# Another order of steps in the later stages of a fused Linformer attention and two-layer kernel on one Trainium2 core

## The chip, the cores and the metric

The kernel runs on one core of one Trainium2 chip. The metric is the device time of one execution in microseconds (us). Engines are called as in the profile: PE (TensorE, matmuls; PEld is its weight loads), DVE (VectorE), ACT (ScalarE), POOL (GpSimd) and SP (SyncE, which here only issues DMAs).

## The reference

Eight batches of an attention with projected keys and values, then two matrix products with a gated activation between them:

```python
k_proj = np.einsum('ks,bhsd->bhkd', E, k)          # b=8, h=8, s=1024, d=64, k=64
v_proj = np.einsum('ks,bhsd->bhkd', F, v)
scores = scale * np.matmul(q, k_proj.transpose(0, 1, 3, 2))
attn = softmax(scores)                              # over the 64 projected keys
x = np.matmul(attn, v_proj)                         # -> (8192 tokens, 512)
h = x @ w_in                                        # 512 -> 2048
g = h * np.clip(h + 3.0, 0.0, 6.0) / 6.0
out = g @ w_out                                     # 2048 -> 512
```

## The kernel before, in words

**Stages.** A batch has 1024 tokens; a stage is 512 of them (t = 0 or 1), so there are 16 stages, named here by batch and t ("5/1" is batch 5, t = 1). Each stage makes the first layer of its own tokens (`g`, 16 blocks of 128 rows) and the second layer of the tokens of the stage ahead of it. The attention of the next batch lies between the matmuls: scores, exponentials and row sums in t = 0, the products with the values in t = 1, and the projection of the batch after that in t = 0.

**Second layer: pairs A and B.** Output rows are made in two pairs, each with seven products of half-size blocks instead of eight (`Pair.step`). A7 is product 7 of pair A, and so on; each is 16 matmuls of 256 columns. Products 7, 2 and 5 go to PSUM tiles `at` and are copied by ACT. Products 6, 1, 3 and 4 add up in this order in one PSUM tile `mm`, and between two of them DVE (ACT after the last) reads the tile into `o_sb`. So the next product of that pair waits for that reading. Product 1 needs the block difference `sb` (DVE), product 3 `sd` (POOL), product 5 `sc` (POOL). N2 and N5 are products 2 and 5 of the next stage's pair A, made a stage early. `o_sb` has three buffers, freed by the store to DRAM.

**First layer from batch 3 on: L0 to L7 and the quarters Q and R.** Half of the blocks of `g` are plain groups (`L` steps, 8 matmuls of 512 columns; ACT makes `r`, DVE makes `g` from `r` and the PSUM tile, line 571). The other half are two quarters made in seven products each (`Quad.step`, 8 matmuls of 256 columns), from sums of `x` blocks that POOL makes (`xc`, `xa`, `xb`, `xd`). Again 6, 1, 3 and 4 add up in one `mm` tile with a DVE subtraction into `qm` (line 136) between them; 7, 2 and 5 go to `at` and are copied by ACT (line 774). Each output goes `qm` -> `r` (ACT, line 783) -> `g` (DVE line 789, or POOL line 787 for products 6 and 1 of R). These parts are put into the queues two steps after the product (`behind_steps(2)`), and the `g` of DVE two more. q3 and q4 are products 3 and 4 of Q, made in the next stage. "gR3" below is the `g` of R3; "gQ1", "gL0" likewise.

**Order.** `QUADS` is the written order of a stage's steps; an engine's work stands in its queue in the order in which the steps issue it. `MADE` says after which step the sums are issued (x: the four sums of x; a: in place in `g`, DVE; b: `sb`; c: `sc`; d: `sd`), `LAST` and `TAIL` are the same for the end, where only the second layer of the last stage is left. The calls of `at(...)` hang the attention onto steps: `scores`, `add_up` (row sums, DVE line 315), `spread` (`sums_turned`, small DVE transposes and adds; `spread_sums`, a DVE reciprocal at line 334 and ten DMAs on SP), `projected` (16 matmuls, then two ACT copies `kp` and, one at each of the next poppable steps, the transposing DMAs on SP and two ACT copies `vp`), and `load_next` (a mark and three DMA issues on POOL).

**PSUM.** There are four `mm` and four `at` tiles; a new tile takes the one that was released longest ago in program order.

The step of a quarter, which the prediction follows most closely (`Quad.step`, without the allocation of its tiles; line 796; `Quad.out` is at line 777, `Pair.step` at line 706, the plan and the loop over the steps from line 856 on):

```python
            self.product(n, self.y if n in (2, 5) else self.x, n in (2, 6))
            if n == 2:
                self.m2 = self.copied("m2", self.y)
            elif n == 5:
                self.m5 = self.copied("m5", self.y)
            elif n == 6:
                sub(self.m7, self.m7, self.x)
                self.out(self.m7, 1, 0, self.engines[0])
            elif n == 1:
                sub(self.m5, self.m5, self.x)
                self.out(self.m5, 1, 1, self.engines[1])
            elif n == 3:
                sub(self.m2, self.x, self.m2)
                self.out(self.m2, 0, 1, self.engines[2])
            else:
                self.out(self.x, 0, 0, nc.vector)
```

Of the kernel before, what the change touches and what calls it, by code (L numbers as in the profile page):

```python
# [15 lines left out]
def kernel(  # L16
# [111 lines left out]
    KH, MH = FO // 2, d_model // 2  # L128
# [100 lines left out]
    class Attention:  # L229
# [38 lines left out]
        def scores(self, j, *allocs):  # L268
            qT = qT_dma[self.b]
            tiles = [alloc() for alloc in allocs]  # L270
            for a in range(2):
                for t in range(NB):
                    for r in range(2):
                        nc.tensor.matmul(tiles[r][t * KP:(t + 1) * KP, a * HT:(a + 1) * HT],  # L274
                                         self.kT[r * D:(r + 1) * D, 2 * j + a, :],
                                         qT[r * D:(r + 1) * D, j, a, t * HT:(t + 1) * HT],
                                         start=True, stop=True)
            return tiles
# [32 lines left out]
        def add_up(self, *js):  # L311
            if self.parts is None:
                self.parts = att.tile([P, KO, 32], f32, tag="parts", name="parts", bufs=1)
            for j in js:
                nc.vector.tensor_reduce(out=self.parts[:, j], op=ALU.add, axis=mybir.AxisListType.X, apply_transpose=True,  # L315
                                        in_=self.aT[j].rearrange("p a r n -> p (a r n)").rearrange(
                                            "p (c i) -> p c i", i=32))
# [283 lines left out]
    xT = x_tile()  # L601
# [235 lines left out]
    for what in "A2 A7 V0 B7 A5 V1 A6 R B2 A1 V2 B5 R A3 B6 V3 A4 B1 R".split():  # L837
# [11 lines left out]
        if what in added:  # L849
            added[what]()  # L850
    xT = x_next
# [3 lines left out]

    ORDER = ("L0 A7 L1 A6 L2 B7 L3 A1 L4 B2 L5 A3 L6 B5 L7 A4 "
             "L8 L9 B6 L10 N2 L11 B1 L12 N5 L13 B3 L14 L15 B4").split()
    QUADS = ("L0 q3 L7 A7 L5 q4 L1 B7 A6 L3 L2 L6 A1 B2 R7 L4 B6 B5 "
             "A3 R2 R6 B1 R5 N2 A4 Q2 R1 Q7 Q6 B3 Q5 R3 Q1 N5 R4 B4").split()
    MADE = {'L1': 'x', 'R2': 'c', 'q3': 'a', 'B2': 'd', 'A6': 'b'}  # L860
    LAST = {'q3': 'ab', 'A6': 'd'}
    ENGINES = ((nc.vector, nc.vector, nc.vector), (nc.scalar, nc.scalar, nc.vector),)
    START = "L0 B3 L1 L2 B4 L3 L4 L5 L6 L7 L8 L9 L10 N2 L11 L12 L13 N5 L14 L15".split()
    TAIL = ("q3 B2 q4 A7 B7 A6 B6 "
             "A1 B5 B1 A3 B3 A4 B4").split()

    second = Attention(2)
# [2 lines left out]
    for b in range(1, B):  # L870
        if b + 1 < B and b < 4:
            x_next = second.xT = x_tile()
        third = Attention(b + 2) if b + 2 < B else None

        plan = {}

        def at(place, *what):
            plan.setdefault(place, []).extend(what)

        def scores(*js):  # L880
            return lambda: second.some_scores(js)

        def values(*js):
            return lambda: second.some_values(*js)

        def add_up(*js):
            return lambda: second.add_up(*js)

        def spread(turned, inverted):
            at(turned, lambda: second.sums_turned())  # L890
            at(inverted, lambda: second.spread_sums())

        if b == 1:
            at((0, "L2"), sums_of_w_in)
            at((0, "L0"), second.projected)
            at((0, "L8"), second.load_next)
            at((0, "N5"), scores(0, 1))
            at((0, "L15"), add_up(0))
            at((1, "L0"), add_up(1))
            at((1, "L1"), scores(2, 3))  # L900
            at((1, "L2"), add_up(2))
            at((1, "L3"), add_up(3))
            spread((1, "B2"), (1, "L5"))
        elif b == 2:
            at((0, "L2"), second.projected)
            at((0, "A4"), second.load_next)
            at((0, "A4"), scores(0, 1))
            at((0, "B6"), scores(2))
            at((0, "L10"), add_up(0))
            at((0, "B1"), scores(3), add_up(1))  # L910
            at((0, "B3"), add_up(2))
            at((1, "A6"), add_up(3))
            spread((1, "A1"), (1, "L4"))
            at((1, "L12"), lambda: sums_in_place(1))
            at((1, "L4"), third.projected)
        elif b + 1 < B:
            if b == 3:
                at((0, "L0"), lambda: sums_in_place(0))
                at((0, "start"), second.load_next)
            at((0, "q3"), scores(0, 1))  # L920
            at((0, "L6"), add_up(0))
            at((0, "L3"), scores(2, 3))
            at((0, "B5"), add_up(1))
            at((0, "R7"), add_up(2))
            at((0, "A4"), add_up(3))
            spread((0, "Q2"), (0, "Q6"))
            if third:
                at((0, "Q2"), lambda: third.projected(pause=False))
                if third.b + 1 < B:
                    at((1, "B1"), third.load_next)  # L930
        if b < 3:
            at((1, "N2"), values(0))
            at((1, "L12"), values(1))
            at((1, "B3"), values(2))
            at((1, "L14"), values(3))
            if b == 1:
                at((1, "B3"), lambda: behind_that(second.recs[1][:1, 0, :1], 3, "q"))
        elif b + 1 < B:
            at((1, "L3"), values(0, 1))
            at((1, "B5"), values(2, 3))  # L940

        def done(place):
            for f in plan.pop((t, place), ()):
                f()

        for t in range(NB):
            if t and 3 < b < B - 1:
                x_next = second.xT = x_tile()
            g = g_tile()
            sums = Sums(g)  # L950
            start = (b, t) == (1, 0)
            pairs = {"A": behind[0], "B": behind[1], "N": Pair(b, t, sums, 0, (b, t) == (B - 1, NB - 1))}
            quads = b > 2
            if quads:
                for i, engines in enumerate(ENGINES):
                    pairs["QR"[i]] = Quad(i, xT, t, g, (b, t) == (B - 1, NB - 1), engines)
            if not start and not quads:
                behind[0].sums.a(KH - left, KH)
            pairs.update({n.lower(): quad for n, quad in before.items()})
            before = {n: pairs[n] for n in "QR" if n in pairs}  # L960
            made = {"a": lambda before=behind[0].sums, lo=KH - left: before.a(lo, KH), "b": behind[0].sums.b,
                    "d": behind[0].sums.d, "c": sums.c, "x": lambda: pairs["Q"].sums(*[pairs[n] for n in "R" if n in pairs])}
            left = 8 if quads else 2
            done("start")
            for what in START if start else QUADS if quads else ORDER:
                n = int(what[1:])

                def sums_made():
                    for op in MADE.get(what, "") if quads else "":
                        made[op]()  # L970

                if what[0] != "L":
                    if what[0] in pairs:
                        pairs[what[0]].step(n)
                    step_done()
                    if quads and what[0] in "LQRB":
                        pop()
                    done(what)
                    sums_made()
                    if what == ("B5" if quads else "N5" if start else "B3") and left < KH:  # L980
                        sums.a(0, KH - left)
                    continue
                if b < 4 and t == 0 and n < 2:
                    if n == 0:
                        first_two = TwoGroups(xT, t, g)
                    for fo in range(2):
                        first_two.part(fo, range(n * (KO - 1), KO - 1 + n))
                    if n == 1:
                        first_two.out()
                else:  # L990
                    first_group(xT, t, g, n, behind_steps(1) if quads and n >= KH else now)
                step_done()
                pop()
                if not quads and n == KH - 1:
                    sums.c()
                if not quads and not start and n == 0:
                    behind[0].sums.b()
                    behind[0].sums.d()
                done(what)
                sums_made()  # L1000
            while soon and not quads:
                step_done()
            behind = [pairs["N"], Pair(b, t, sums, 1, (b, t) == (B - 1, NB - 1))]
        assert not plan, plan
        second, xT = third, x_next
# [40 lines left out]
```

## Time and profile before

| what | us |
|---|---|
| median of 3 runs (lowest to highest) | 485.64 (485.25 to 485.98) |
| the profiled execution | 486.51 |
| its span, first to last instruction | 484.7 |
| PE busy in the span | 472.8 (98%) |
| DVE busy | 368.6 (76%) |
| ACT busy | 299.1 (62%) |
| POOL busy | 266.6 (55%) |

The granted TensorE clock is 1.00 in every stretch. The first `L0` of batch 3 starts at 191.14, that of 3/1 at 220.95, of 4/0 at 249.18, 4/1 at 277.51, 5/0 at 305.73, 5/1 at 334.07, 6/0 at 362.29, 6/1 at 388.90, 7/0 at 416.78 and 7/1 at 442.64; the tail starts at 468.50, and the last matmul at 480.52 ends it.

A row of the timeline gives the start, the time taken, the engine, the line, the operation, what it writes and reads, and how many instructions the row merges; in brackets stands the idle time ahead of it and who ended it. A matmul row's end is modelled, and the next row may start before it; the distance between the starts of two steps is what a step costs.

### The profile page before, as it was taken

How to read it: one execution, taken by the hardware profiler on the slowest of the kernel's cores; microseconds unless marked ns; L12 is line 12 of the kernel's file. 1: busy time of each engine (PE TensorE's matmuls, PEld its weight loads, DVE VectorE, ACT ScalarE, POOL GpSimd, SP SyncE). 2: the span in 40 equal slices, each digit the busy share in tenths (PEclk: the TensorE clock that was granted, in tenths of full speed). 3: DMA queues.
4: the chain of work that ended last, by engine and by line, in shares of the span. 5: the costliest groups of instructions: out<-in, count | busy, mean ns of one | idle time of the engine just before them, and what ended most of it. 6: DMA issues, size and time to landing. Idle time of an engine off the chain costs nothing.

```text
span 484.7 us, 15486 instructions
## 1 busy us (share of the span) xinstructions
PE 472.8 (98%) x6690; PEld 357.1 (74%) x6690; DVE 368.6 (76%) x578; ACT 299.1 (62%) x580; POOL 266.6 (55%) x175
## 2 busy tenths in 40 slices
PE   8999999999999999999999999999999999999996
PEld 3554567667676786687788868787697968888896
DVE  3582386678856858879879797998979997968784
ACT  2666587774357454757486755867468665757471
POOL 8624948244135333865694648575475657576510
PEclk9999999999999999999999999999999999999999
DMA  9999999984986969988699495966810171101012
GB/s 164 198 201 207 230 157 210 182 127 92 245 130 119 212 155 217 193 184 152 165 167 184 107 167 137 201 128 124 200 65 23 69 197 47 46 34 57 23 69 88
DMA packets 84597, 68.70 MB, mean 142 GB/s; under 512 B 38320, under 2 KB 70576, under 8 KB 84528
## 3 DMA queue, kind: packets, MB, share of 16 engines
q0 software_dynamic: 33008, 29.36, 39.2%
q1 hardware_dynamic: 51152, 37.83, 32.0%
q8 instruction: 52, 0.85, 0.8%
q10 hardware_dynamic: 368, 0.52, 0.4%
q14 instruction: 17, 0.14, 0.1%
HBM read 71.83 MB, written 16.97 MB: 183 GB/s over the span
## 4 chain that ended last, share of the span: by engine, by line
PE 66%; DVE 18%; DMA 5%; POOL 4%; ACT 3%; issue 2%; SPq 1%; DVEq 0%; ACTq 0%; POOLq 0%
PE mm L206 44%; PE at L206 17%; DVE g L789 5%; DVE g L571 4%; DVE qm L136 2%; DVE g L136 1%; DVE sb L136 1%; PE at L295 1%; DMA qT<-q 1%; DMA g<-in_F_dram 1%; DVE parts L315 1%; DVE o_sb L136 1%; PE at L274 1%; DMA rec<-turned_rows 1%; DVE xT L307 1%
## 5 line engine op out<-in xcount | busy, mean ns | idle before, releaser
L206 PE MATMUL mm<-xT,w_in_sb 128*64 128x512 bf16 (+1 forms) x1568 | 183.5, 369 | 1.6 <-ACT o_sb L738 0.9
L206 PEld LDWEIGHTS <-w_in_sb 128*64 128x64 bf16 x2048 | 116.4, 110 | 58.7 <-issue 9.9
L571 DVE SCALAR_TENSOR_TENSOR g<-r,mm 128x512 bf16<-128x512 f32 x176 | 117.6, 680 | 46.8 <-ACT r L570 46.0
L570 ACT ACTIVATE r<-mm 128x512 f32<-128x512 f32 x176 | 104.4, 598 | 70.6 <-PE mm L206 55.4
L206 PEld LDWEIGHTS <-g 128*64 128x64 bf16 x2048 | 113.4, 110 | 20.8 <-issue 3.6
L136 POOL TENSOR_TENSOR sd<-g,sb 128x1024 bf16<-128x1024 bf16 x28 | 59.0, 2127 | 80.6 <-DVE sb L136 80.6
L133 POOL TENSOR_TENSOR sc<-g 128x2048 bf16<-128x2048 bf16 x14 | 57.0, 4072 | 46.5 <-DVE g L571 34.1
L206 PE MATMUL mm<-w_out_sb,g 128*64 128x256 bf16 (+1 forms) x1088 | 77.7, 285 | 1.0 <-DVE o_sb L136 0.7
L206 PE MATMUL at<-w_sums,g 128*64 128x256 bf16 x896 | 59.2, 273 | 0.0
L700 ACT COPY m<-at 128x256 f32<-128x256 f32 x84 | 31.1, 370 | 33.7 <-PE at L206 29.1
L774 ACT COPY qm<-at 128x512 f32<-128x512 f32 x60 | 34.9, 582 | 25.0 <-PE at L206 18.2
L783 ACT ACTIVATE r<-qm 128x512 f32<-128x512 f32 x60 | 37.8, 630 | 12.3 <-DVE qm L136 12.2
L789 DVE SCALAR_TENSOR_TENSOR g<-r,qm 128x512 bf16<-128x512 f32 x42 | 42.5, 1027 | 2.1 <-ACT r L783 1.9
L136 DVE TENSOR_TENSOR qm<-qm,mm 128x512 f32<-128x512 f32 x40 | 27.3, 686 | 19.6 <-PE mm L206 15.4
L307 DVE TENSOR_TENSOR xT<-at,rec 128x512 bf16<-128x512 f32 x54 | 35.9, 682 | 3.7 <-PE at L295 1.7
L787 POOL TENSOR_TENSOR g<-r,qm 128x512 bf16<-128x512 f32 x18 | 22.9, 1274 | 28.0 <-ACT r L786 27.9
L206 PE MATMUL mm<-w_sums,sb 128*64 128x256 bf16 x480 | 31.4, 273 | 1.3 <-DVE sb L136 1.0
L206 PE MATMUL mm<-w_out_sb,sd 128*64 128x256 bf16 x480 | 31.6, 273 | 1.1 <-POOL sd L136 1.0
L283 ACT ACTIVATE aT<-at 128x512 bf16<-128x512 f32 x52 | 29.3, 598 | 1.9 <-PE at L274 1.9
L206 PEld LDWEIGHTS <-sb 128*64 128x64 bf16 x480 | 26.2, 110 | 5.7 <-DVE sb L136 2.6
L315 DVE TRANSPOSE_TENSOR_REDUCE parts<-aT 128x32 f32<-128x1024 bf16 x24 | 29.6, 1232 | 0.0
L206 PE MATMUL at<-w_out_sb,sc 128*64 128x256 bf16 x448 | 29.4, 273 | 0.0
(115 smaller groups left out, 613.2 us busy)
## 6 DMA issues: line engine op xcount, KB each, us to landing
out_dram<-o_sb SPq DMA_DIRECT2D x60, 256.0 KB, 3.8
rec<-turned_rows SPq DMA_DIRECT2D x48, 256.0 KB, 6.2
k<-in_k_dram POOLq DMA_DIRECT2D x7, 1024.0 KB, 9.7
v<-in_v_dram POOLq DMA_DIRECT2D x7, 1024.0 KB, 15.3
q<-in_q_dram POOLq DMA_DIRECT2D x7, 1024.0 KB, 19.4
w_out_sb<-in_moe_w_out_dram POOLq DMA_DIRECT2D x4, 512.0 KB, 14.8
w_in_sb<-in_moe_w_in_dram POOLq DMA_DIRECT2D x7, 256.0 KB, 9.4
k<-in_k_dram POOLq DMA_DIRECT2D x4, 256.0 KB, 5.8
```

The costliest lines, as they stand in the source:

```text
L133: engine.tensor_tensor(out=out, in0=x, in1=y, op=ALU.add)
L136: engine.tensor_tensor(out=out, in0=x, in1=y, op=ALU.subtract)
L206: nc.tensor.matmul(ps[lo:lo + width], stationary[:, lo:lo + width], moving, **flags)
L283: when(lambda r=r: nc.scalar.activation(aT[:, :, r, :], tiles[r].rearrange("p (a n) -> p a n", a=2), AF.Exp, scale=scale))
L307: when(lambda t=t: nc.vector.tensor_mul(self.xT[:, j, t, :], av[t], rec[:, t]))
L315: nc.vector.tensor_reduce(out=self.parts[:, j], op=ALU.add, axis=mybir.AxisListType.X, apply_transpose=True, in_=self.aT[j].rearrange("p a ...
L570: nc.scalar.activation(r, h_ps, AF.Relu, bias=0.5, scale=1.0 / 6.0)
L571: when(lambda: nc.vector.scalar_tensor_tensor(g[:, fo, :], r, 1.0, h_ps, op0=ALU.min, op1=ALU.mult))
L700: self.copy(m, ps)
L774: nc.scalar.copy(m, y)
L783: nc.scalar.activation(r, h, AF.Relu, bias=0.5, scale=(-1.0 if engine is nc.scalar and not self.last else 1.0) / 6.0)
L789: behind_steps(2)(lambda: nc.vector.scalar_tensor_tensor(g, r3, 1.0, h3, op0=ALU.min, op1=ALU.mult))
```

## The change

It gives another written order to the stages of batches 3 to 7 and to the tail, and hangs sums and attention onto other steps:

```diff
-    QUADS = ("L0 q3 L7 A7 L5 q4 L1 B7 A6 L3 L2 L6 A1 B2 R7 L4 B6 B5 "
-             "A3 R2 R6 B1 R5 N2 A4 Q2 R1 Q7 Q6 B3 Q5 R3 Q1 N5 R4 B4").split()
-    MADE = {'L1': 'x', 'R2': 'c', 'q3': 'a', 'B2': 'd', 'A6': 'b'}
-    LAST = {'q3': 'ab', 'A6': 'd'}
+    QUADS = ("L0 q3 L7 A7 L5 q4 L1 B7 A6 L3 L2 L6 A1 B6 B2 L4 R7 B5 "
+             "R6 R2 B1 A3 R5 Q2 R1 Q7 N2 Q6 A4 R3 B3 Q5 Q1 N5 R4 B4").split()
+    MADE = {'L6': 'x', 'R6': 'c', 'A6': 'b', 'q3': 'a', 'R7': 'd'}
+    LAST = {'q3': 'ab', 'B5': 'd'}
...
-    TAIL = ("q3 B2 q4 A7 B7 A6 B6 "
+    TAIL = ("q3 A7 B2 B7 B6 q4 A6 "
              "A1 B5 B1 A3 B3 A4 B4").split()
...
-            at((0, "q3"), scores(0, 1))
-            at((0, "L6"), add_up(0))
-            at((0, "L3"), scores(2, 3))
-            at((0, "B5"), add_up(1))
-            at((0, "R7"), add_up(2))
-            at((0, "A4"), add_up(3))
-            spread((0, "Q2"), (0, "Q6"))
+            at((0, "L0"), scores(0, 1))
+            at((0, "B6"), add_up(0))
+            at((0, "L6"), scores(2, 3))
+            at((0, "R6"), add_up(1))
+            at((0, "L6"), add_up(2))
+            at((0, "A3"), add_up(3))
+            spread((0, "Q7"), (0, "Q7"))
             if third:
-                at((0, "Q2"), lambda: third.projected(pause=False))
+                at((0, "R5"), lambda: third.projected(pause=False))
                 if third.b + 1 < B:
-                    at((1, "B1"), third.load_next)
+                    at((1, "A3"), third.load_next)
...
-                    if what == ("B5" if quads else "N5" if start else "B3") and left < KH:
+                    if what == ("R2" if quads else "N5" if start else "B3") and left < KH:
...
-                    first_group(xT, t, g, n, behind_steps(1) if quads and n >= KH else now)
+                    first_group(xT, t, g, n, behind_steps(2) if quads and n >= KH else now)
```

The first line of the last two edits is in force only where `left < KH`; with the quarters `left` is 8 and `KH` is 8. The second is in force only for `n >= 8`, and `QUADS` holds L0 to L7 alone. Neither alters an instruction. The number and the shapes of the matmuls stay as they are.

## The prediction

> **What bounds the kernel now.** First the page: PE is busy nearly all the time. (Measured against the runs shown, 0.2%, about 1.0 us, is what can be told from no change.)
>
> ```profile
> span 484.7 us, 15486 instructions
> PE 472.8 (98%) x6690; PEld 357.1 (74%) x6690; DVE 368.6 (76%) x578; ACT 299.1 (62%) x580; POOL 266.6 (55%) x175
> ```
>
> So the order can win only what PE waits. Then I walked PE's timeline from batch 3 on and took the distance between the starts of successive steps. Undisturbed, a pair product or an L group takes 0.87 and a quarter product 0.44 (5/0: starts at 321.42, 322.30, 322.73). What is over is lost:
>
> - 5/1: L0 0.06, q3 (L7 comes late) 0.49, A7 (L5 late) 0.48, B2 (R7 late) 0.24, together 1.27; 3/1 and 4/1 the same.
> - 3/0: 1.13 ahead of A1 and 1.19 within A3. 6/1: 0.28 (L5), 0.30 (A6), 0.33 (R7). 7/0 and 7/1: 0.58 each (half ahead of A1). Tail: 0.27, 0.38 (B1) and 0.89 (B4).
>
> Some 9.8 us in all; switches to attention matmuls (0.1 each) and 0.31 in each `values(2, 3)` stay. The Trainium skill (Trainium Kernel Development and Optimization, Performance Expectations) calls matmul busy time a bad metric, because matmuls are pipelined. The trace agrees: from 200 us on the busy time leaves only 5.2 us idle ahead of the last matmul, less than the sum over starts.
>
> Now who holds PE up at the start of a t = 1 stage; PE, then DVE, then ACT in the same stretch:
>
> ```profile
> 334.07 1.03 PE L206 MATMUL mm<-xT,w_in_sb 128*64 128x512 bf16 x8
> 335.00 0.63 PE L206 MATMUL mm<-xd,w_in_sb 128*64 128x256 bf16 x8
> 335.92 1.05 PE L206 MATMUL mm<-xT,w_in_sb 128*64 128x512 bf16 x8 [0.29 <-ACT o_sb L738]
> ```
> ```profile
> 329.11 0.69 DVE L136 TENSOR_TENSOR qm<-qm,mm 128x512 f32<-128x512 f32 x1 [1.19 <-PE mm L206]
> 330.17 0.69 DVE L136 TENSOR_TENSOR qm<-qm,mm 128x512 f32<-128x512 f32 x1 [0.38 <-ACT qm L774]
> 330.78 0.94 DVE L334 RECIPROCAL inv<-inv 64x128 f32<-64x128 f32 x1
> ...
> 334.87 2.61 DVE L789 SCALAR_TENSOR_TENSOR g<-r,qm 128x512 bf16<-128x512 f32 x2
> ```
> ```profile
> 334.98 0.63 ACT L783 ACTIVATE r<-qm 128x512 f32<-128x512 f32 x1 [0.39 <-DVE qm L136]
> 335.51 0.35 ACT L738 COPY o_sb<-mm 128x256 f32<-128x256 f32 x1
> ```
>
> L7 needs the tile that B4 leaves; B4's copy on ACT (335.51) stands behind the `r` of Q1, which waits for the subtraction after Q1 on DVE. DVE then has gR3 and gQ1 (334.87 to 337.48) ahead of gL0, whose tile L5 needs. DVE is late there because R3, Q5 and Q1 come close together, and in 4/1 ACT's copy after Q5 waits 0.87 for POOL's gR1, which holds the one `qm` buffer of product 5. Two more waits:
>
> ```profile
> 204.45 4.21 POOL L136 TENSOR_TENSOR sd<-g,sb 128x1024 bf16<-128x1024 bf16 x2
> ...
> 208.72 0.63 PE L206 MATMUL mm<-w_out_sb,sd 128*64 128x256 bf16 x8 [0.99 <-POOL sd L136]
> ```
> ```profile
> 480.04 0.42 DVE L136 TENSOR_TENSOR o_sb<-mm,m 128x256 f32<-128x256 f32 x1 [1.50 <-DMA out_dram<-o_sb]
> 480.52 1.06 PE L206 MATMUL mm<-w_out_sb,g 128*64 128x256 bf16 x16 [0.69 <-DVE o_sb L136]
> ```
>
> **Part by part.** Matmuls are the same, so each part is worth the wait that it adds or ends.
>
> *Sums (x, d, c) at other steps: nothing.* On POOL the order stays x, sd, sc, gR6, gR1; x still runs as soon as gR1 and Q5 are done, sd when `sb` is.
>
> *A3 three steps later (behind R6, R2, B1).* In 3/0 POOL reaches sd late (it ends at 208.6). A3 would start at 202.30 + 4x0.87 (A1, B6, B2, L4) + 0.44 (R7) + 0.87 (B5) + 2x0.44 + 0.87 = 208.8: the 1.19 go. The 1.13 ahead of A1 stay: `sb` (3.18 us beside x on POOL) does not move.
>
> *B6 and B2 ahead of L4 and R7.* R7 comes 1.7 us later against the `at` tile that it waits for, and B2 0.9: 0.24 gone in 3/1 to 5/1, 0.33 in 6/1. B6 now needs the `mm` tile of L3 0.9 to 1.7 us earlier; in 4/1 gL3 ends at 288.9 and B6 would start at 289.6: hidden.
>
> *Two-step distances.* Between two products on one tile PE in the stages now has at least 2.2 us of other steps (B3 to B4), where R3 to R4 had 1.3; a DVE reading is 0.33 to 0.68. R1 to Q5 grows from 2.2 to 4.4 us, so ACT's wait for gR1 goes. R6 to Q7 shrinks from 4.4 to 3.9 (more with the projection between): gR6 stands behind sc (4.07) on POOL, and in 7/0 ACT's copy after Q7 waits 1.1 us, with r of R1 and m of N2 behind it; Q6's subtraction is then ready 0.4 later, and Q1 three steps after: nothing for PE.
>
> *Scores, row sums, projection.* scores(0, 1) ahead of q3 instead of behind it cost PE the same 0.56. add_up(2) now stands on DVE right behind scores(2, 3) and waits for two exponentials (0.35 us), with the readings of A1 and B6 behind it, whose next products are 9 and 7 steps off: hidden. The projection at R5 puts its transposes (SP) ahead of A4's store, which now also stands behind the row sums' ten DMAs: the transposes would run from 327.4 to 333.1 and the ten DMAs 7.6 us more (280.30 to 287.91 in 4/1), so it leaves near 341 and lands near 345; its buffer is next written after B6 of the next stage, near 347. load_next after A3 is 0.9 later on POOL, still ahead of gR1, for data used a stage later.
>
> *End of a t = 0 stage (5/0, with PE's times as they would be: R1 ends at 327.0, Q6 at 328.8, Q1 starts at 331.35, the next L0 at 334.0).* Now sums_turned and the reciprocal stand together ahead of Q6's subtraction. DVE from 327.15 without a pause: subtraction after R1 0.60, sums_turned 2.0, reciprocal 0.86, after Q6 0.60 (ends 331.2), after R3 0.60, B3's reading 0.33, gQ6 1.1, after Q1 0.60 (ends 333.8), gR3 1.2, gQ1 1.25: 336.3, where before it was 337.5. ACT's r of Q1 can then run at 333.9, B4's copy ends at 334.8, and L7 wants it at 335.3: 0.49 and L0's 0.06 gone. gL0 ends at 336.9, L5 wants its tile at 337.05. That has no room, so I take half of 0.48. With R7's 0.24 each of 3/1, 4/1 and 5/1 gains 1.03. In 6/0 there is no projection, so PE is there 1.7 us sooner while DVE is not: gQ1 ends 2.55 after the next L0 (2.6 before), so 6/1 keeps all but R7's 0.33; and Q6's subtraction ends 0.1 after Q1 wants to start, 0.2 lost.
>
> *7/0 and 7/1.* At the end of 6/1 nothing of the row sums is in the way: gQ1 ends 1.2 after L0 instead of 2.3, at the end of 7/0 1.8 instead of 2.3; `sb` follows on a DVE without a pause, so A1's wait (0.27) and the ones ahead go: 0.48 and 0.38 of 0.58.
>
> *Tail.* A1 now follows A6 at once and must wait for A6's reading: 0.6 lost. q4 later puts its `g`, and so sd on DVE, behind A1's reading: A3 waits 0.35. But A1's reading no longer stands behind sd (476.04 to 476.41 before), and its store, on whose buffer B3's reading waits, leaves 0.7 sooner; such a store took 3.6 (to 480.04). B4 would end 12.3 after the start of the tail, not 12.9: 0.55 gained.
>
> Sum: 1.19 + 3x1.03 + (0.33 - 0.2) + 0.86 + 0.55 = 5.8 us. The profiled execution (486.51; span 484.7 and 1.8 around it) is 0.87 over the median; the gains are taken from the median: 485.64 - 5.8 = 479.8. Everything that could go gone, 7.9 us, gives 477.7.
>
> **Rivals.**
>
> *DVE stays late (25%).* x starts on POOL 1.1 us sooner against the stage's end, so three DVE operations meet it. Rows: gR3 and gQ1 take 2.42 to 2.61 beside POOL's x, 1.47 at 467.96 with POOL idle. If each is held to the end of a whole POOL operation (1.60) and then takes its own 0.60, DVE's chain ends some 2.8 us later and the stage starts keep their stalls: 1.19 + 3x0.24 + 0.33 + 0.55 = 2.8 gained, 482.9. The Trainium skill (SBUF — State Buffer, Who interferes with whom) gives this rule: a DVE instruction with two SBUF inputs and a GpSimd one that reads SBUF exclude each other for the whole instruction. The rows above show 1.2 each, so less than the worst case.
>
> *Slower: the block of row sums (15%).* 2.86 us of DVE work stand ahead of Q6's subtraction, and Q1 cannot start before that. In 3/0 to 5/0 DVE has 1.3 us to spare ahead of R1, in 6/0 none. From there every us by which DVE falls behind (four add_ups of 1.15 now between L6 and R5, the first behind the exponentials) is a us of PE in each of four stages, and the stage starts stay late. With 1.2 us: 485.64 - 2.8 + 4x1.2 = 487.6; it decides from 0.7 us on. Against it: the chain above, worked out from 5/0's own rows.
>
> *No difference (5%).* The waits only move to the next tile: 485.6.
>
> **Numbers.** The main case has 55%; 479.8 is its time, 477.7 to 482 its own range. Faster by over 0.2% is it and the first rival: 0.80; same 0.05, slower 0.15. The range from 477.9 to 485.0 takes in both, and leaves out the slower rival and a few per cent below.
>
> **What would show it.** In the changed profile: A3 of the first quarter stage without a wait for sd; L7 and L5 of t = 1 stages 0.87 apart from their neighbours; no ACT wait for POOL's gR1; a wait of about 0.6 between A6 and A1 in the tail. Wrong: waits of Q1 for DVE's `qm` in t = 0, or L7 and L5 waiting as now.

## The result and the profile after

The changed kernel takes 491.97 us (median of six runs, 489.43 to 494.18), the kernel before 486.15 in the runs beside it (485.25 to 488.11): the ratio is 1.0117, with a 95% interval of 1.0077 to 1.0158. It is slower by some 5.7 us, where a gain of 5.8 was forecast. The profiled execution took 490.93.

Page of the changed kernel (span, the busy times, the granted clock in 40 slices, then one of the costliest groups and one of the DMA issues):

```profile
span 489.1 us, 15494 instructions
PE 472.5 (97%) x6690; PEld 360.7 (74%) x6690; DVE 367.1 (75%) x578; ACT 298.4 (61%) x580; POOL 265.7 (54%) x175
...
PEclk9999999999999999999899999999989999999999
...
L136 DVE TENSOR_TENSOR o_sb<-m,mm 128x256 f32<-128x256 f32 x60 | 24.1, 408 | 15.6 <-DMA out_dram<-o_sb 9.5
...
out_dram<-o_sb SPq DMA_DIRECT2D x60, 256.0 KB, 4.7
```

PE's busy time is what it was (472.5 against 472.8), so by this page the difference is idle time. A matmul at half clock counts as busy all the same (from 356.63 to 360.04 PE is busy for all of the 3.41 us, at a granted clock of 0.50), so part of it can be slow clock. The group on `o_sb` names a wait of 9.5 us for a DMA (1.5 before, all of it in the tail), the stores' median from issue to landing is 4.7 us (3.8 before), and the clock has two dents. The waits of DVE say how often (total, times, longest):

```profile
DVE o_sb L136 <- DMA out_dram<-o_sb: 9.5, 3, 3.7
```

Three times, one in each of 3/1, 4/1 and 5/1. Counted from the start of one step to the start of the next, as the prediction does, PE loses 5.32 us in 3/1 (2.12 before), 2.84 in 4/1 (2.10) and 5.60 in 5/1 (2.11), and from 191 us to the end 19.8 (15.3). The difference of 4.5 is that of the spans (4.4). Here is 3/1, first DVE's timeline, then PE's:

```profile
231.70 0.69 DVE L307 TENSOR_TENSOR xT<-at,rec 128x512 bf16<-128x512 f32 x1
232.31 0.41 DVE L136 TENSOR_TENSOR o_sb<-m,mm 128x256 f32<-128x256 f32 x1
236.13 0.42 DVE L136 TENSOR_TENSOR o_sb<-m,mm 128x256 f32<-128x256 f32 x1 [3.41 <-DMA out_dram<-o_sb]
236.47 0.68 DVE L307 TENSOR_TENSOR xT<-at,rec 128x512 bf16<-128x512 f32 x1
```
```profile
234.06 0.40 PE L295 MATMUL at<-aT,vp 64*64 64x512 bf16 x2
237.20 1.06 PE L295 MATMUL at<-aT,vp 64*64 64x512 bf16 x6 [2.74 <-DVE xT L307]
238.20 1.06 PE L206 MATMUL mm<-xa,w_in_sb 128*64 128x256 bf16 x8
239.05 1.06 PE L206 MATMUL at<-xT,v_sums 128*64 128x256 bf16 x8
239.90 1.37 PE L206 MATMUL mm<-w_sums,sb 128*64 128x256 bf16 x16
...
241.98 0.60 PE L206 MATMUL at<-xc,w_in_sb 128*64 128x256 bf16 x8
242.42 0.60 PE L206 MATMUL at<-xT,v_sums 128*64 128x256 bf16 x8
```

The reading after B6 wants to write an `o_sb` buffer that a store has not yet emptied. It stands at the head of DVE, so the `xT` of `values(2, 3)` stands behind it, and PE's attention matmuls wait for the `at` tile which that `xT` reads. PE names `xT`, DVE names the store. (Behind the wait R6 and R2, the rows at 238.20 and 239.05, cost 0.85 each, and R5 at 241.98 again the usual 0.44: that is the clock, of which more below.) The cause is one row deeper, in the SP queue. First SP of the changed kernel from the end of 3/0 into 3/1, then of the kernel before (start, time on the queue, DMAs):

```profile
212.28 1.21 SPq L257 DMA_TRANSPOSE kT<-kp  x1
215.36 5.73 SPq L194 DMA_TRANSPOSE qT<-q  x2
221.19 1.00 SPq L337 DMA_DIRECT2D turned_rows<-inv  x2
223.34 5.16 SPq L343 DMA_DIRECT2D rec<-turned_rows  x8
228.59 4.49 SPq L704 DMA_DIRECT2D out_dram<-o_sb  x3
```
```profile
213.71 0.33 SPq L704 DMA_DIRECT2D out_dram<-o_sb  x1
216.57 1.22 SPq L257 DMA_TRANSPOSE kT<-kp  x1
```

Before, A4's store leaves at 213.71, ahead of everything. Now it is the first of the three that leave from 228.59 on, behind three transposes, the two DMAs that write the turned rows and the eight that read them back to all partitions. And it lands late, at 236.0. The DMA view of the changed kernel from 226 to 242 (busy share in 40 slices of 0.4 us) shows why:

```profile
DMA  8999995889999999999999986310000100000000
```

The eight transfers of 256 KB fill the DMA engines until 235.6; the store issued behind them lands 0.4 us later.

### The profile page after: what moved, and what is told of

It is laid out like the page before. It is cut to its first block, busy times and chain, and to the rows that moved or that the text cites. A ratio compares the mean times of both kernels' runs of the same rounds, so it can differ in the third digit from the quotient of the medians.

```text
span 489.1 us, 15494 instructions
## 1 busy us (share of the span) xinstructions
PE 472.5 (97%) x6690; PEld 360.7 (74%) x6690; DVE 367.1 (75%) x578; ACT 298.4 (61%) x580; POOL 265.7 (54%) x175
## 4 chain that ended last, share of the span: by engine, by line
PE 78%; DVE 7%; DMA 7%; ACT 4%; POOL 2%; issue 2%; ACTq 0%; DVEq 0%; POOLq 0%
PE mm L206 55%; PE at L206 19%; DMA out_dram<-o_sb 5%; DMA v<-in_v_dram 2%; PE at L295 2%; DVE g L571 2%; DVE g L789 2%; PE at L274 1%; ACT aT L283 1%; DVE parts L315 1%; DVE qm L136 1%; DVE sb L136 1%; POOL q L103 1%; DVE o_sb L136 1%; ACT r L570 1%
## 5 line engine op out<-in xcount | busy, mean ns | idle before, releaser
L789 DVE SCALAR_TENSOR_TENSOR g<-r,qm 128x512 bf16<-128x512 f32 x42 | 45.3, 1089 | 1.8 <-ACT r L783 1.4
L136 DVE TENSOR_TENSOR o_sb<-m,mm 128x256 f32<-128x256 f32 x60 | 24.1, 408 | 15.6 <-DMA out_dram<-o_sb 9.5
L206 PE MATMUL mm<-w_sums,sb 128*64 128x256 bf16 x480 | 32.6, 280 | 0.9 <-DVE o_sb L136 0.5
```

Of the source, the lines that this page charges most:

```text
L136: engine.tensor_tensor(out=out, in0=x, in1=y, op=ALU.subtract)
L206: nc.tensor.matmul(ps[lo:lo + width], stationary[:, lo:lo + width], moving, **flags)
L789: behind_steps(2)(lambda: nc.vector.scalar_tensor_tensor(g, r3, 1.0, h3, op0=ALU.min, op1=ALU.mult))
```

## The experiments

Theory S is this one: the new place of A4 and of the projection on SP delays A4's store, and the wait for its buffer is the whole loss. Theory K adds that the longest of these waits cost more than their length, since PE's clock falls after them. The rivals, which go by further letters where an expectation names them, are the other new waits that the change could have made: row sums that reach `values(2, 3)` too late, the transposes or the new plan of attention as such, the new order of the products. All ratios are to the kernel before, run on the same chip.

**1. A4's store past SP's queue.** In the changed kernel the store of A4 in t = 0 is issued from ACT.

```diff
+            self.queue = nc.sync
...
-                self.store(0, left if self.final else slice(0, d_model), nc.scalar if self.final else nc.sync)
+                self.store(0, left if self.final else slice(0, d_model), nc.scalar if self.final else self.queue)
...
+                        if quads and t == 0 and what == "A4":
+                            pairs["A"].queue = nc.scalar
                         pairs[what[0]].step(n)
```

> The changed kernel, but in the t = 0 stages the store of A4's rows is issued from ACT's queue instead of SP's. Theory S (the store stands on SP behind the projection's three transposes and the row sums' ten DMAs, so its o_sb buffer comes free late, DVE's reading after B6 of the next stage waits 2.4 to 3.6 us, and PE runs dry at values(2, 3) and then at half clock): those waits and the half clock go, about 12 us of the changed kernel's 491 to 492; about 480, ratio to before 0.985 to 0.992. Rival V (the products with the values wait for their own reciprocals, which the moved row sums bring late): within 1 us of the changed kernel, 491. Rival O (B6 ahead of L4 as such, not the buffer): 490 to 492.

Measured: 481.84 us (480.41 to 482.38), ratio 0.9909 (0.9884 to 0.9934). The wait for `o_sb` is gone, and the clock is 0.999 for the whole span of 480.6. One queue for one store turns the loss into a gain: S holds, and the rivals have nothing left of the loss to explain. What remains of them in the stretch of the loss is 1.02 us on DVE in 3/1, where `xT` waits for `rec`, and 0.64 of it reaches PE.

**2. The late store alone, in the kernel before.** Only the store of A4 moves there, to behind Q6.

```diff
+                send = lambda: self.store(...)
+                send() if self.kept is None else self.kept.append(send)
...
+                        if quads and t == 0 and b < B - 1 and what == "A4":
+                            pairs["A"].kept = []
...
+                    if quads and t == 0 and b < B - 1 and what == "Q6":
+                        for send in pairs["A"].kept:
+                            send()
```

> The kernel before, with one edit: in the t = 0 stages of batches 3 to 6 the store of A4's rows is issued after Q6, behind the row sums' DMAs, and not at A4. Theory S: it leaves SP as late as in the changed kernel (some 9 us after the next L0 and 7 to 8 us to landing), but B6 is 1.7 us later in this order, so DVE's reading waits 0.7 to 1.9 us and part of it reaches PE: 487 to 490, ratio 1.003 to 1.010, the wait of o_sb for the DMA seen in 3/1, 4/1 and 5/1. Rivals V and O: no change, 485.6 to 486.2, ratio 0.998 to 1.002.

Measured: 488.86 (486.79 to 490.05), ratio 1.0051 (1.0032 to 1.0071). The waits of DVE:

```profile
DVE o_sb L136 <- DMA out_dram<-o_sb: 7.1, 4, 2.9
```

One of the four is the tail's old one. At the step behind A3, which needs the tile that the `xT` behind the wait reads, PE loses 0.42, 1.93 and 0.86 in 3/1, 4/1 and 5/1, 3.2 in all, which is near what the ratio gives (2.5 us). The late store is enough to make the kernel before slower, with no other part of the change.

**3. The projection behind A4.** In the changed kernel its transposes are issued at A4, so that the store goes ahead of them.

```diff
-                at((0, "R5"), lambda: third.projected(pause=False))
+                at((0, "A4"), lambda: third.projected(pause=False))
```

> The changed kernel with the projection hung onto A4 instead of R5, so that its three transposes stand on SP behind A4's store; the row sums' ten DMAs stay ahead of it. Theory S: the store leaves 6 to 8 us sooner, the wait goes in all three stages: 480 to 482, ratio 0.986 to 0.993. Rival D (not the queue, but the row sums' broadcasts in flight make the store land in 7.5 us instead of 3.8): a wait of 1 us or more stays in 3/1 to 5/1, 484 to 489. Rival V: 491.

Measured: 480.82 (480.27 to 481.51), ratio 0.9893 (0.9871 to 0.9916), span 478.6. SP, in the place shown above:

```profile
222.26 0.54 SPq L704 DMA_DIRECT2D out_dram<-o_sb  x1
```

The store leaves 6.3 us sooner and no reading waits for it, though it still takes 6.7 us to land, behind the same eight transfers. The transposes are as many as before and run later still (the `qT` ones from 224.30 to 232.33), so they do no harm by themselves.

**4. The row sums behind A4.** The other half of the queue: the reciprocal and the ten DMAs of the row sums move from Q7 to R3, behind A4, while the projection stays at R5.

```diff
-            spread((0, "Q7"), (0, "Q7"))
+            spread((0, "Q7"), (0, "R3"))
```

> The changed kernel with the reciprocal and the row sums' ten DMAs hung onto R3 instead of Q7, so that they stand behind A4's store (and DVE reads Q6 ahead of the reciprocal); the transposes stay ahead. Theory S: the store leaves at the end of the transposes, about 7 us sooner, the wait goes: 480 to 481, ratio 0.986 to 0.992. Rival D: the same. Rival V (reciprocals late): the row sums come later still, so 491 or more.

Measured: 481.18 (480.30 to 481.92), ratio 0.9896 (0.9868 to 0.9924). The store leaves at 221.38, now ahead of the eight transfers, and lands in 2.8 us. To clear either half out of its way is enough. The row sums are read back later here than in the changed kernel (from 224.65 instead of 223.34), and the loss is gone all the same: late row sums are not its cause. They are not free either: DVE's `xT` waits for `rec` three times, 3.1 us in all, and 3/1 takes 28.05 us from L0 to L0, where experiment 3 has 27.23.

**5. The order without the plan.** The changed orders and sums with the hooks of the kernel before, except for `add_up(3)`, which stays at A3.

```diff
-            at((0, "L0"), scores(0, 1))
+            at((0, "q3"), scores(0, 1))
...
-                at((0, "R5"), lambda: third.projected(pause=False))
+                at((0, "Q2"), lambda: third.projected(pause=False))
```

> The changed order of steps, sums and tail with the attention of the kernel before on its old steps (projection and sums_turned at Q2, reciprocal and row DMAs at Q6, scores at q3 and L3; add_up(3) at A3, since A4 now comes after Q2). Theory S: A4 still comes after both, so its store still stands behind transposes and row DMAs: the wait of o_sb for the DMA stays in 3/1, 4/1 and 5/1, 487 to 492, ratio 1.003 to 1.013. Rival P (the new places of the projection and the row sums cause the loss): as fast as with the store freed, 480 to 482.

Measured: 489.88, 491.05 and 493.80, ratio 1.0105 (1.0067 to 1.0143). The fourth execution, the profiled one, took 1236 us and is left out, so there is no trace to read. The new orders and sums are enough for a loss of that size. Theory S has the reason: in the new order A4 stands behind Q2 and Q6, at which that plan puts the projection and the row sums on SP, where in the kernel before it stood ahead of both. That it is the store which costs the time in this run is not shown.

**6. The plan without the order.** The kernel before with the changed hooks.

```diff
-            spread((0, "Q2"), (0, "Q6"))
+            spread((0, "Q7"), (0, "Q7"))
...
-                at((0, "Q2"), lambda: third.projected(pause=False))
+                at((0, "R5"), lambda: third.projected(pause=False))
```

> The kernel before with the new places of the attention alone (scores, add_up, projection at R5, row sums at Q7, load_next at A3), order, sums and tail as before. Theory S: A4 still comes ahead of Q2, where the transposes are issued, and of Q7, so its store leaves in time: no wait of o_sb for a DMA in t = 1; the stage starts wait as before: 485 to 487, ratio 0.998 to 1.003. Rival P (the new places as such cause the loss): 489 to 492, ratio 1.007 to 1.013.

Measured: 487.54 (486.68 to 488.65), ratio 1.0026 (1.0009 to 1.0043). There is no wait for a store in t = 1, but another one appears in each of 3/0 to 6/0, 4.4 us in all. PE and then DVE in 4/0:

```profile
275.81 0.63 PE L206 MATMUL mm<-xb,v_sums 128*64 128x256 bf16 x8 [1.09 <-DVE qm L136]
```
```profile
274.27 0.94 DVE L334 RECIPROCAL inv<-inv 64x128 f32<-64x128 f32 x1
275.14 0.62 DVE L136 TENSOR_TENSOR qm<-qm,mm 128x512 f32<-128x512 f32 x1
```

This is the prediction's slower rival, the block of row sums ahead of Q6's subtraction: 4/0, 5/0 and 6/0 take 1.25 us longer from L0 to L0 than in the kernel before. It exists in the old order, where 1.75 us of other steps lie between Q6 and Q1; in the new one there are 2.6, and no Q1 waits. The ratio lies in the range of theory S (the time, 487.54, is 0.5 above it), but the stage starts do not wait as before, as S had said: 3/1, 4/1 and 5/1 are 1.0 us shorter each and 6/1 0.8, which takes most of the new waits back.

**7. B6 later.** In the changed kernel B6 goes behind B2, L4 and R7, some 2.2 us later, where the buffer is asked for later.

```diff
-    QUADS = ("... A1 B6 B2 L4 R7 B5 "
+    QUADS = ("... A1 B2 L4 R7 B6 B5 "
```

> The changed kernel with B6 moved behind R7 (A1 B2 L4 R7 B6 B5), nothing else: DVE's reading after B6, which waits for the buffer, is asked for 2.2 us later, and the store is as late as in the changed kernel. Theory S: the waits of 2.4 to 3.6 us shrink by 2.2 each, PE waits at most 1.5 us in a stage and keeps its full clock: 482 to 485, ratio 0.992 to 0.998. If the loss came from the store's lateness through another reader than B6's: 490 to 492.

Measured: 483.73 (481.65 to 486.60), ratio 0.9949 (0.9921 to 0.9977). The waits of DVE keep 3.6 us for the store in two places, where 9.5 in three were:

```profile
DVE o_sb L136 <- DMA out_dram<-o_sb: 3.6, 2, 2.0
```

Two of the three waits are left, and shorter: it is a race between landing and asking, and either end moves it. The runs whose mean clock is 0.999 or 1.000 take 481.65 to 483.73, those at 0.996 take 484.8 to 486.6.

**8. The wait kept, the clock kept up.** Fourteen matmuls of no use ahead of `values(2, 3)` in 3/1 and 5/1, so that PE is not idle while it waits for the store.

```diff
+            if b in (3, 5):
+                at((1, "B5"), lambda: busy(14))
             at((1, "B5"), values(2, 3))
```

> The changed kernel with 14 idle matmuls of 128x512 (about 3.0 us, results unused) put ahead of values(2, 3) in 3/1 and 5/1, where PE waits about 2.9 us. Theory K (a wait of 2.7 us and more halves PE's clock for 3.41 us, 1.7 us each, on top of the wait): the matmuls fill the wait, the clock stays at 1.00 there and 3 to 4 us are gained on the changed kernel: 487 to 489, and the runs lie closer together. Without K: no gain or a loss of up to 1 us, 491 to 493.

Measured: 489.21 (488.85 to 490.41), ratio 1.0061 (1.0046 to 1.0076). The windows view from 229 to 245 us (length, busy time of PE, PEld, DVE, ACT and POOL, then the granted clock, the DMA share and GB/s), of the changed kernel and then of this one:

```profile
229.00:245.00 16.00, 13.26 (x196) 11.05 (x194) 9.85 (x18) 6.35 (x13) 11.07 (x7) 0.89 0.50 141
```
```profile
229.00:245.00 16.00, 15.94 (x231) 12.66 (x230) 10.85 (x20) 7.56 (x15) 11.38 (x7) 1.00 0.50 135
```

With the idle time filled (PE's busy time here holds the matmuls of no use) the clock stays at 1.00, and about half of the slowdown is gone though the store is as late (DVE still waits for it three times, 9.0 us in all): K holds. The time is 0.2 above the range that K gave. The difference of the two ratios is 0.56%, some 2.7 us; their intervals leave 0.6 to 4.8 for it. Two half-clock stretches of 3.41 us are worth 3.4, if PE loses half of each.

**9. What is left, mended.** Three versions, each built on the last. The first has the projection at A4 (experiment 3), `load_next` at Q7 of t = 1, `values(2, 3)` at R6 and A6 ahead of B6 in the tail:

```diff
-    TAIL = ("q3 A7 B2 B7 B6 q4 A6 "
+    TAIL = ("q3 A7 B2 B7 A6 q4 B6 "
...
-                    at((1, "A3"), third.load_next)
+                    at((1, "Q7"), third.load_next)
...
-            at((1, "B5"), values(2, 3))
+            at((1, "R6"), values(2, 3))
```

> The changed kernel with four edits: projection at A4 (as in the run with the projection behind), load_next at Q7 (so that POOL's gR1 does not stand behind three DMA issues; waits at q3 and L7 of 4/0 and 5/0, 0.8 each), values(2, 3) at R6 (behind the copy after B5, 0.3 in each of four stages), and A6 two steps ahead of A1 in the tail (0.7 + 0.2). If the four add up: 480.8 - 1.6 - 1.2 - 0.9 = 477.1, ratio 0.980 to 0.985. If the waits only move on: 480 to 481, ratio 0.988 to 0.990.

Measured: 480.86 (480.16 to 481.29), ratio 0.9880 (0.9864 to 0.9897). Two edits worked: 4/0 and 5/0 lose 0.52 each where experiments 1, 3 and 4 lost 1.3 to 1.9, and the tail 0.48 instead of 1.07. The third took it back, so that the time is that of the other forecast, in which the waits only move on: with `values(2, 3)` at R6, R2 waits for `xT` and loses 1.06 in each of four stages, where B5's place cost 0.4.

The second puts `values(2, 3)` back at B5:

> The run with all four edits, but values(2, 3) left at B5: at R6 it made R2 wait 1.06 for DVE's products in each of four stages, against 0.41 at B5. So 4x0.65 = 2.6 sooner: 478.3, ratio 0.981 to 0.985. If that wait only moves: 480 to 481, ratio 0.988.

Measured: 478.13 (476.90 to 479.19), ratio 0.9829 (0.9801 to 0.9857).

The third goes at the wait ahead of A1 in 3/0, which no part of the change touched:

```diff
-                at((0, "L0"), lambda: sums_in_place(0))
+                at((0, "start"), lambda: sums_in_place(0))
                 at((0, "start"), second.load_next)
```

> The run before this one (three edits), and in 3/0 POOL makes the two in-place sums of w_in ahead of the mark and the three DMA issues of load_next, so that the four sums of x run about 2 us sooner and less beside DVE's sb (2.97 us there, 1.2 alone): of A1's wait of about 1.0 half goes: 477.8, 0.1% less than the run without it; under what the runs can tell from it unless the trace shows sb shorter. If sb is as slow: the same, 478.3.

Measured: 477.25 (476.94 to 477.72), ratio 0.9813 (0.9787 to 0.9839); 3/0 loses 0.49 instead of 1.47. It has the lowest median of all, 9 us below the kernel before. By time alone it can't be told from the second version (476.94 to 477.72 against 476.90 to 479.19); the wait that is gone is in the trace.

## Why the prediction was wrong, step by step

**The step that failed** is in "Scores, row sums, projection". It saw that the projection at R5 puts the transposes ahead of A4's store and the row sums' DMAs too, and worked out that the store leaves near 341, 7 us after the next L0 (334.0), lands near 345 and is asked for near 347: 2 us of room, hidden. Three terms of that sum against what came, counted from the next L0:

- It leaves at +9.7, +8.5 and +10.1 (3/1, 4/1, 5/1) instead of +7. In 5/1 the transposes start where the prediction had them (330.73 for L0 at 337.29), but hold the queue for 7.1 us instead of 5.7, and the rows' ten DMAs for 9.5 (7.4 and 9.0 in 3/1 and 4/1) instead of 7.6. The 7.6 was read in 4/1; in 5/1, the stage that the sum is about, the kernel before had 9.3 already (335.52 to 344.81). What differs is how long the read-back waits for the two row writes: it starts 2.4, 2.5 and 4.1 us after the first of them in 3/1, 4/1 and 5/1 of the kernel before, and 2.2, 3.8 and 4.3 now.
- It lands 7.3 to 7.6 us after it leaves instead of 3.8. That was the median over all 60 stores; this one goes behind 2 MB that still occupy the DMA engines. This term alone is more than the room there was, and it too stood in the trace of the kernel before: there the stores that leave right behind the ten DMAs, at 231.08 in 3/1 and at 344.91 in 5/1, land after 7.6 and 7.5 us, but no reading waits for them. The DMA view of the first:

```profile
out_dram<-o_sb SPq DMA_DIRECT2D x1, 256.0 KB, 7.6
```

- It is asked for at +13.8 to +13.9 instead of +13, which helps by 0.9.

So 2.0 us of room became waits of 3.4, 2.4 and 3.7. The prediction took a wait as hidden on a margin of 2 us between two estimates, and gave no rival to it: the two rivals that had a mechanism were both on DVE. And it priced a wait by its length: behind the two longest the clock was halved as well.

**What held.** With the store out of the way the total of the sum is there. Experiment 3 has the change's every other part and a ratio of 0.9893 (0.9871 to 0.9916); the forecast was 479.8 / 485.64 = 0.9880. Its span is some 10.5 below the changed kernel's: from L0 to L0, 3/1, 4/1 and 5/1 are 4.2, 2.0 and 4.7 us shorter, and the other stages 0.5 longer together. That the total fits so well is in part luck. Against the kernel before, experiment 3 gains 7.4 us in the stages of which the prediction expected 5.8 (3/0 1.6 instead of 1.19; 3/1, 4/1 and 5/1 3.5 instead of 3.1; 6/1, 7/0 and 7/1 1.8 instead of 1.0; the tail 0.5), and loses 1.6 in 4/0 and 5/0, for which the prediction had nothing (see `load_next` below).

- *End of a t = 0 stage.* L7 and L5 of 5/1 now come without a wait (L0, q3, L7, A7 and L5 start 0.86, 0.44, 0.86 and 0.95 apart: 0.08 lost ahead of L5, 0.48 before):

```profile
337.29 1.03 PE L206 MATMUL mm<-xT,w_in_sb 128*64 128x512 bf16 x8
338.15 0.60 PE L206 MATMUL mm<-xd,w_in_sb 128*64 128x256 bf16 x8
338.59 1.03 PE L206 MATMUL mm<-xT,w_in_sb 128*64 128x512 bf16 x8
339.45 1.04 PE L206 MATMUL at<-w_sums,g 128*64 128x256 bf16 x16
340.40 1.92 PE L206 MATMUL mm<-xT,w_in_sb 128*64 128x512 bf16 x20
```

  The chain behind it fits: B4's copy starts at L0 + 0.5 and ends at L0 + 0.86 (predicted 0.8), gQ1 ends at L0 + 2.46 (2.3; before 3.4). `sums_turned` took 1.4 instead of 2.0, so L5 had room where only half of its wait was taken as gone. At these stage starts the rival "DVE stays late" did not come; the 0.2 taken for Q1 in 6/0 did not either.
- *A3.* Right: sd ends at 207.76 on POOL, A3 starts at 207.95 with no wait. The wait ahead of A1, which was said to stay, shrank too, from 1.13 to 0.46 (scores(2, 3) stand ahead of A1 now and take 1.02 instead of the usual 0.56).
- *6/1, 7/0 and 7/1.* 6/1 loses 1.15 instead of 1.77 (0.33 was expected to go), 7/0 and 7/1 lose 0.02 each instead of 0.63 and 0.64 (0.48 and 0.38 were).
- *Tail.* The new wait of A1 for A6's reading is there, 0.69 start to start (0.6 predicted), A3 loses 0.16 ahead of it and 0.2 within it (0.35), and B3's reading waits for no store. The tail's loss goes from 1.57 to 1.07, a gain of 0.5 (0.55 predicted):

```profile
479.29 1.06 PE L206 MATMUL mm<-w_sums,sb 128*64 128x256 bf16 x16 [0.52 <-DVE o_sb L136]
```

- *load_next, and the rival "DVE stays late".* `load_next` was said to stay ahead of gR1 and given no price. It does stay there: its three DMA issues (0.9 each) stand directly ahead of gR1, as they did before. But R3 comes 1.3 us sooner against the end of the stage in the new order, and gR3 on DVE now meets gR1 and the sums of x that follow it on POOL. POOL, then DVE, at the end of 4/1:

```profile
304.65 1.31 POOL L787 TENSOR_TENSOR g<-r,qm 128x512 bf16<-128x512 f32 x1
305.89 1.17 POOL L133 TENSOR_TENSOR xc<-xT 128x512 bf16<-128x512 bf16 x1
307.00 1.17 POOL L136 TENSOR_TENSOR xa<-xT 128x512 bf16<-128x512 bf16 x1
```
```profile
305.08 3.65 DVE L789 SCALAR_TENSOR_TENSOR g<-r,qm 128x512 bf16<-128x512 f32 x1
```

  gR3 takes 3.65 us, where it took 0.95 in the kernel before (at 303.93), and ends 0.56 behind xa. That is what the rival describes, an operation held to the end of POOL's and then its own 0.60, only through three of them and ahead of a t = 0 stage: 5/0 loses 1.88 (0.49 before). In experiments 1, 3 and 4 gR3 takes 3.1 to 3.6 us ahead of 4/0 and of 5/0, and both stages lose 1.3 to 1.9; in the changed kernel it is short ahead of 4/0, which loses 0.48. The second version of experiment 9 differs from experiment 3 in the place of `load_next` and in the tail alone: no gR3 is held there, and 4/0 and 5/0 take 28.3 us each instead of 29.1 and 29.2. ACT's wait for gR1, which was to go, is there as before: 4.7 us in five waits, 5.2 in six in the kernel before.

Left open: how the 10.5 us divide. The three waits and what stands behind them at full clock would be some 7, the two half-clock stretches 3.4; experiment 8 measures the second part only to within 0.6 and 4.8.

## What to carry to other kernels

A DMA moved on a queue moves everything behind it, and a store is also the release of its buffer: follow it from its place in the queue, through what still occupies the DMA engines when it leaves, to the next writer of the buffer, and take each time from a row in the same surroundings, not from another stage or from the median. Where the slack is smaller than the sum of the errors of its terms, it is a rival with a price. Here two waits of under 3 us on the busiest engine cost more than their length, so look at the granted clock behind a wait.

## What the runs showed that was not expected

PE's clock falls after quite a short pause. After 2.74 us of waiting in 3/1 and 2.94 in 5/1 the record shows half clock for 3.41 us, and R6 and R2 in 3/1 take 0.85 from start to start where 0.44 is usual; after 1.66 us in 4/1 it stays at 1.00. The length of the pause need not be all that counts. In 3/1 the half clock begins at 237.16, with PE's next matmuls, in 5/1 at 356.63, 0.8 us behind them, and the 119.47 us between the two are 35 times 3.413, the length of a stretch. That looks like a fixed grid of such windows, each followed by half clock if PE did too little in it: in the windows ahead of the two stretches PE is busy for 0.72 and 0.76 us, in the two that share the wait of 4/1 for 2.46 and 2.69. By that reading the same pause can halve the clock in one run and not in the next. Two stretches in one trace do not settle it.

A stretch that falls where PE is what the kernel waits for costs 1.7 us, half of its length, and the number of stretches fits the spread of the changed kernel's runs: one makes a mean clock of 0.9965, and the run at 0.997 took 489.43, the three runs at 0.993 (two stretches) 490.93 to 492.56, those at 0.990 and 0.986 (three and four, by that count) 494.18 and 494.12. The count is rough, and not every dip costs time: a run of the kernel before at 0.995 took 485.85, no more than its neighbours (their median is 485.81).

The Trainium skill (TensorE: Matmul & The Clock Gate, "Why this matters for your kernels") asks for no PE-idle gaps over about 3 us; here one of 2.74 us was enough. The Trainium skill names a window of 3.4 us on the same page ("What's actually happening"), and the length of the stretches agrees with it.

And in these rows DVE and POOL take turns by whole instructions. In 3/0, DVE's `sb` (two inputs in SBUF) and POOL's sums of x, in the version before the last and in the last one:

```profile
198.96 3.00 DVE L136 TENSOR_TENSOR sb<-g 128x2048 bf16<-128x2048 bf16 x1
```
```profile
198.60 1.16 POOL L133 TENSOR_TENSOR xc<-xT 128x512 bf16<-128x512 bf16 x1
199.72 1.15 POOL L136 TENSOR_TENSOR xa<-xT 128x512 bf16<-128x512 bf16 x1
200.94 2.03 POOL L136 TENSOR_TENSOR xb<-xT,xa 128x512 bf16<-128x512 bf16 x1
```
```profile
198.76 1.22 DVE L136 TENSOR_TENSOR sb<-g 128x2048 bf16<-128x2048 bf16 x1
```

In the first, `sb` stands until xc and xa are through (200.87) and then takes its 1.1, for which xb stands 0.9 longer; in the last one POOL's sums run 3.2 us sooner, `sb` meets the end of one of them, and A1 no longer waits. The rows of gR3 in 5/0, above, are a longer case. The Trainium skill (SBUF — State Buffer, Who interferes with whom) states the rule, that the one which holds the shared pair keeps it for its whole instruction. The prediction set it aside as a worst case; here the rows agree with it, and by the durations xa went ahead of an `sb` that already stood there (xc and xa ahead of gR3 in 5/0), which is more than the rest of one instruction.
